# A gated long-convolution/MLP kernel on one core: sines before the filter copies, taps in one evacuation, zero matmuls on the idle TensorE, and even transforms evacuated into their own target

## Chip, cores, metric

The kernel runs on one core of a Trainium2 chip. The metric is the device time of one execution in microseconds. Each time of a kernel below is a median over several executions, slow ones included; what is said of points within a kernel comes from one profiled execution. Ratios are the mean time of one kernel's fast runs over the mean of the fast runs of the kernel before from the same rounds, with a 95% interval, so they are not quite the ratio of the medians that stand beside them. The span of a profile (first to last instruction) is about 2 us shorter than the time of the same run. A run is called slow where it is more than 1.5% above the fastest of the same kernel.

## The reference, cut to what matters

```python
x = A_q                                             # [1, 2048, 640]
g = sigmoid((x * gate_w).sum(-1, keepdims=True))
# A: 4-tap shift of k, times v, long convolution over 2048 rows with a filter per column, times q
k_shift = sum over t of k_pad[:, t:t + S] * shift_k[:, ks - 1 - t]
kv = k_shift * v
y = irfft(rfft(kv, 2S) * rfft(ssm_k, 2S))[:S] + kv * ssm_D
a = q * y
# B: MLP over the token axis
h = layernorm(x)
u = gelu(einsum("bsd,sf->bdf", h, w1) + b1)          # F = 1536
b = einsum("bdf,fs->bds", u, w2) + b2
return g * a + (1 - g) * b
```

The transform is made of matmuls with twiddle tables. The filter `ssm_k`, the product `kv` and the inverse all go through it; the MLP's first layer (512 KB loads of weights into `ring`, `X` as the other operand) and second layer (768 KB loads into `W`) fill TensorE between and behind the transforms.

## The kernel before: the parts that matter

The program is a list of operations with modelled durations. A list scheduler plays them through and fixes the order on each engine and queue; the order is then emitted, with semaphores worked out from the data dependencies. Its priorities and its `after` edges shape only the order. So a wrong duration in the model does no harm to correctness, but an engine takes its instructions in the planned order, and what the plan puts ahead goes first (in the profile after, a GELU evacuation stands behind a copy that waits 12.96 us). All matmuls are issued on one helper line (L293), all ScalarE activations on another (L667), and I tell them apart by their tiles.

The model of a DMA is short:

```python
if e in ("SP", "QA") or op.lat < 0:
    issue = 1.2 if e == "POOL" else 0.1
    s = max(t + issue, dma_free)
    dma_free = s + op.dur                      # bytes / rate, one transfer after the other
    op.end = dma_free + 2.0 + (6.0 if e == "POOL" else 0.0)
```

The front: twiddle angles (`pint`, VectorE), their sines (`FTB`, ScalarE), the filter blocks (`ssm`) transposed on TensorE and copied out (`wT`, ScalarE), the taps (`cw`), then the filter transform in 16 groups of four matmuls, each copied out by ScalarE into `C`. LayerNorm statistics of `X` follow on VectorE, and the tap matrix `KF` on GpSimd.

```python
for p in PORD:                                       # (0, 2, 1, 3)
    tt("DVE", pv, acol[p], brow, ALU.mult)           # angles as integers
    ts("DVE", pint[:, p, :, 0, :], pv, 1024.0, None, ALU.add)
    ts("DVE", pa, pa, 4095, None, ALU.bitwise_and)
    act(FTB[:, p], pa, ACT.Sin, ...)                 # cut
```

The transforms of `kv`: the even residues are evacuated into slots of another buffer (`Th`), VectorE adds them into the target, and the mixing follows.

```python
def fwd_even(src, h, dst, Th, Ts):
    for p in (0, 2): ...                             # 8 groups of two matmuls
        act(V(Th, Ts * SL + D * pos[(p, kt, c)], ...), two, ACT.Copy, vt=vt, name="Ae")
    tt_("DVE", V(dst, 0, ...), t4(0, ...), t4(2, ...), ALU.add)        # three additions
```

The middle, for the inverse transform: four DMA transposes, one for each residue `p`, read `FTB` and write `GTB`, and ScalarE gathers each back into `FTB` once the forward transforms have used that residue. `GTB` shares memory with the gate's products `gq`. The second layer's weights (`W`) are loaded on the same queue (SP).

```python
for p in range(4):
    dma(GTB[:, p], FTB[:, p], 128 * 2048, rate=200.0, transpose=True, prio=10 ** 5)
    act(V(FTB, 1024 * p, ...), V(GTB, 1024 * p, ...), ACT.Copy, prio=10 ** 5, name="gil")
for n_, hk in enumerate(HORD):
    for a in range(2):
        w2last = dma(W2h[:, 6 * a:6 * a + 6, :], dr(B_w2, ...), 128 * 6144)
```

Of the kernel before, what the change touches and what calls it, by code (L numbers as in the profile page):

```python
# [9 lines left out]
BF16 = mybir.dt.bfloat16  # L10
# [313 lines left out]
class _Sched:  # L324
# [59 lines left out]
    def run(self):  # L384
# [13 lines left out]
        free = {e: 0.0 for e in engs}  # L398
# [112 lines left out]
def _build(nc, A_q, A_k, A_v, A_shift_k, A_ssm_k, A_ssm_D, B_x, B_w1, B_b1, B_w2, B_b2, gate_w, out):  # L511
# [10 lines left out]
    with ExitStack() as es:  # L522
# [73 lines left out]
        rows = alloc("rows", [20, 4, 512], BF16, at=base_of(GT))  # L596
# [169 lines left out]
        small(rows[0:20, 0, 0:128], dr(A_shift_k, 0, [[128, 20], [1, 128]]), 5120, "QA")  # L766
        small(rows[0:4, 1, :], dr(B_b2, 0, [[512, 4], [1, 512]]), 4096, "QA")
        small(rows[0:12, 2, 0:128], dr(B_b1, 0, [[128, 12], [1, 128]]), 3072, "QA")
        for a, b in SSM0:
            ssm_load(0, a, b)  # L770
        for hk in range(4):
            x_load(hk)
        for a, b in SSM1:
            ssm_load(1, a, b)
        w1_load(0, 0)
        w1_load(0, 1)

# [9 lines left out]
        memset("POOL", cw[:, :, :], 0.0)  # L787
        ro, ri = rows[0:20, 3, :].rearrange("g (j q c) -> g j q c", j=4, q=4), V(rows, 0, [[1, 4], [0, 4], [4, 32]], pn=20)
        SC.add("DVE", 0.6, lambda s: T.op("DVE", lambda e: e.tensor_copy(ro, ri), [ri], [ro]), [ri], [ro], prio=0, name="taps")
        PORD = (0, 2, 1, 3)  # L790
        for p in PORD:
            pv = pint[:, p, :, 1, :]
            tt("DVE", pv, V(acol, p, [[4, 2], [0, 256]]), V(brow, 0, [[0, 2], [1, 256]]), ALU.mult, mode=1)
            ts("DVE", pint[:, p, :, 0, :], pv, 1024.0, None, ALU.add, mode=2)
            pa = pint[:, p, :, :, :].rearrange("q a b c -> q (a b c)")
            ts("DVE", pa, pa, 4095, None, ALU.bitwise_and, mode=2)
            act(FTB[:, p, :, :, :, :].rearrange("q a b c d -> q (a b c d)"), pa, ACT.Sin, bias=cst[:, 0:1],
                scale=-(2.0 * math.pi / 4096.0) * (1.0 - 1e-6), name="sin")
# [9 lines left out]
        for j in range(4):  # L808
            items.append(((lambda s, j=j: s[:, 512 + 20 * j:512 + 20 * j + 20]), rows[0:20, 3, 128 * j:128 * j + 128], ident[0:20, 0:20], True, True))
        mms(vt, items, prio=0, name="cst")  # L810
        for q in range(4):
            act(V(cw, q, [[7, NG], [1, 4]], p0=32 * q, pn=32), (lambda s, q=q: s[32 * q:32 * q + 32, 512:592].rearrange("p (j g) -> p g j", j=4)), ACT.Copy, vt=vt, prio=0, name="cw")
        b2f = V(cc, 0, [[1, 4], [4, 4]])
        ts("DVE", dif2[:, :], dif2[:, :], 31, None, ALU.bitwise_and, mode=2)
        ts("DVE", m32[:, :], dif2[:, :], 0.0, None, ALU.is_equal, mode=2)
# [10 lines left out]
        def transp(h, db):  # L826
            vt = _VT("cv")
            items = []
            for kt in range(2):
                for p in range(4):  # L830
                    o = (lambda s, j=4 * kt + p: s[:, 128 * j:128 * j + 128])
                    dfold = h == 0 and kt == 0 and p == 0
                    if dfold:
                        items.append((o, ident[0:1, :], Drow[0:1, 128 * db:128 * db + 128], True, False))
                    items.append((o, V(ssm, db * S + 1024 * h + 4 * kt + p, [[8, 128]]), ident[:, :], not dfold, True))
            mms(vt, items, name="wtr")
            act(V(wT, 2 * h * SL + 128 * db, [[SL, 2], [D, 4], [1, 128]]), (lambda s: s[:, :].rearrange("q (a b c) -> q a b c", a=2, b=4)), ACT.Copy, vt=vt, name="wT")

        def fwd(src, h, p, dst, slot, scale, name, neg=lambda c, k2: False):
            for k2 in range(2):  # L840
                for c in range(2):
# [5 lines left out]
                    mms(vt, items, name=name)  # L847
# [5 lines left out]
        def fwd_even(src, h, dst, Th, Ts):  # L853
            pos = {(0, 0, 0): 0, (0, 0, 1): 1, (0, 1, 0): 2, (0, 1, 1): 3, (2, 0, 1): 4, (2, 1, 0): 5, (2, 1, 1): 6, (2, 0, 0): 7}
            for p in (0, 2):
                for kt in range(2):
                    for c in range(2):
                        vt = _VT("cv")
                        items = [(chk(ci), FTB[:, p, kt, c, 0, :], src(kt, p, ci), True, True) for ci in range(2)]
                        mms(vt, items, name="A")  # L860
                        act(V(Th, Ts * SL + D * pos[(p, kt, c)], [[320, 2], [1, 320]]), two, ACT.Copy, vt=vt, name="Ae")

            def t4(o, n, dims):
                return V(Th, Ts * SL + D * o, dims + [[1, n]])
            tt_("DVE", V(dst, 0, [[2 * D, 2], [1, D]]), t4(0, 2 * D, []), t4(2, 2 * D, []), ALU.add)
            tt_("DVE", V(dst, 2 * SL + 2 * D, [[-2 * D, 2], [1, D]]), t4(4, 2 * D, []), t4(6, 2 * D, []), ALU.add)
            tt_("DVE", V(dst, D, [[2 * SL, 2], [2 * D, 2], [1, D]]), t4(0, D, [[4 * D, 2], [D, 2]]), t4(2, D, [[4 * D, 2], [D, 2]]), ALU.subtract)
# [53 lines left out]
        for h in range(2):  # L921
# [4 lines left out]
            for p in PORD:  # L926
                fwd(srcW(h), h, p, C[h], p, 1.0 / 1024.0, "W", (lambda c, k2: False) if h == 0 else (lambda c, k2: c == 1))
            if h == 0:
# [14 lines left out]
                for g0 in KFP:  # L943
                    tt("POOL", KF[:, g0:g0 + 20 // len(KFP), :, :], V(cw, 7 * g0, [[7, 20 // len(KFP)], [1, 7], [0, 32]]), V(m32, 0, [[0, 20 // len(KFP)], [0, 7], [1, 32]]), ALU.mult)
# [54 lines left out]
        fwd_even(srcA, 0, C[2], C[1], 0)  # L999
# [6 lines left out]
        fwd_even(srcB, 1, C[3], C[2], 0)  # L1006
# [252 lines left out]
```

## Time and profile before

| | |
|---|---|
| time, median | 190.22 us of the three runs that the prediction had (189.38 to 190.36); 190.00 with a fourth; 189.8 to 190.6 in the rounds of the experiments |
| span of the profile | 187.7 us |
| TensorE / VectorE / ScalarE / GpSimd busy | 93% / 90% / 64% / 20% |
| first filter matmul | 15.99 us |
| first MLP matmul | 25.54 us |
| `kv` matmuls begin | 48.41 us |
| last GELU evacuation begins | 115.28 us |

How it is read (page, chain, front, clock) stands in the prediction. This is the SP queue of the kernel before, from 70 to 110 us (start, length, line, operation and tile), and beneath it, in a second fence, how long its four transposes took to land:

```profile
79.80 13.61 SPq L260 DMA_TRANSPOSE GTB<-FTB  x4
93.45 1.20 SPq L267 DMA_DIRECT2D W<-in_B_w_dram  x2
```

```profile
DMA to landing us min/median/max: 3.0/3.2/4.7
```

### The profile page before, as it was taken

To read this page: it belongs to the slowest core of one execution; us is meant where nothing else is said; L and a number is where in the kernel's file an instruction comes from. 1 tells how busy PE (TensorE), PEld (TensorE's weight loads), DVE (VectorE), ACT (ScalarE), POOL (GpSimd) and SP (SyncE) were. 2 spreads that over 40 slices of the span, in tenths; PEclk is the share of its full clock that TensorE was granted. 3 is DMA by queue.
4 is the path that set the end of the run, shared out by engine and by line. 5 is a ranking of instruction groups with operands and counts; after the bars stand their busy time and mean duration, and the time that the engine had idled before them with its cause. 6 is when DMAs were issued, how large, how long until landed. Compare 5 with 4: busy or idle time off the path is not lost.

```text
span 187.7 us, 3316 instructions
## 1 busy us (share of the span) xinstructions
PE 173.7 (93%) x1374; PEld 129.7 (69%) x1374; DVE 168.7 (90%) x199; ACT 119.4 (64%) x180; POOL 36.9 (20%) x41
## 2 busy tenths in 40 slices
PE   3746999989999999999979999999999999999994
PEld 2523668756877786767747777888888887778673
DVE  7899795999499963999999999999999999969974
ACT  2996889599987999999798111231313224563760
POOL 2089304000000550000011530200204131252000
PEclk9999999999999999999999999999999999999999
DMA  5999999999991899990699599965967999999453
GB/s 168 400 409 370 386 218 230 365 415 193 200 338 50 196 209 231 232 201 0 132 224 271 107 191 159 341 119 170 325 124 226 303 202 248 259 211 227 138 211 138
DMA packets 38206, 42.85 MB, mean 228 GB/s; under 512 B 15787, under 2 KB 31280, under 8 KB 38192
## 3 DMA queue, kind: packets, MB, share of 16 engines
q1 hardware_dynamic: 33200, 32.15, 56.6%
q0 software_dynamic: 4928, 10.49, 31.6%
q8 instruction: 10, 0.16, 0.4%
q14 instruction: 4, 0.03, 0.0%
q10 hardware_dynamic: 64, 0.01, 0.0%
HBM read 25.87 MB, written 2.62 MB: 152 GB/s over the span
## 4 chain that ended last, share of the span: by engine, by line
PE 81%; ACT 15%; DMA 1%; issue 1%; DVE 0%
PE pp L293 81%; ACT C L667 4%; ACT wT L667 4%; ACT FTB L667 3%; ACT ksh L667 2%; DMA ssm<-in_A_ssm_k_dram 1%; ACT L667 1%; ACT GT L667 1%; ACT cw L667 0%; DVE O L679 0%; ACT gth L667 0%
## 5 line engine op out<-in xcount | busy, mean ns | idle before, releaser
L623 DVE TENSOR_TENSOR C<-C 128x2560 bf16<-128x2560 bf16 (+2 forms) x34 | 52.2, 1565 | 6.8 <-ACT C L667 6.8
L293 PE MATMUL pp<-X,ring 128*128 128x320 bf16 x384 | 55.4, 299 | 1.5 <-ACT GT L667 1.2
L293 PE MATMUL pp<-GT,W 128*128 128x320 bf16 x384 | 52.8, 299 | 0.0
L293 PEld LDWEIGHTS pp<-GT,W 128*128 128x128 bf16 x384 | 43.4, 114 | 8.8 <-ACT cgb L667 0.2
L293 PEld LDWEIGHTS pp<-X,ring 128*128 128x128 bf16 x384 | 37.2, 98 | 16.5 <-issue 1.9
L667 ACT ACTIVATE C<-pp 128x640 bf16<-128x640 f32 x64 | 40.4, 718 | 6.1 <-PE pp L293 6.0
L667 ACT ACTIVATE O<-pp,c,omg 128x640 bf16<-128x640 f32 x15 | 13.3, 884 | 34.7 <-PE pp L293 34.7
L293 PE MATMUL pp<-wT,FTB 128*128 128x320 bf16 x128 | 21.3, 323 | 2.2 <-ACT wT L667 1.4
L293 PEld LDWEIGHTS pp<-wT,FTB 128*128 128x128 bf16 x128 | 12.6, 104 | 9.7 <-ACT wT L667 1.5
L262 POOL DMA_DIRECT2D C<-C x8 | 9.9, 1359 | 47.3 <-DVE C L623 47.1
L667 ACT ACTIVATE GT<-pp,cc 128x640 bf16<-128x640 f32 x12 | 9.5, 792 | 13.0 <-PE pp L293 12.9
L262 POOL DMA_DIRECT2D C<-q_hi x6 | 5.9, 984 | 54.5 <-DVE C L623 27.6
L667 ACT ACTIVATE cgb<-pp,gg 128x640 bf16<-128x640 f32 x16 | 12.7, 794 | 5.7 <-PE pp L293 5.7
L623 DVE TENSOR_TENSOR tm<-C,C 128x2560 bf16<-128x2560 bf16 (+1 forms) x7 | 14.4, 2057 | 0.0
L899 DVE BATCH_NORM_STATS2 stats<-X 128x6 f32<-128x320 bf16 x32 | 13.4, 460 | 0.6 <-DMA X<-in_A_q_dram 0.6
L293 PE MATMUL pp<-C,FTB 128*128 128x320 bf16 x96 | 13.7, 299 | 0.0
L623 DVE TENSOR_TENSOR C<-tm 128x2560 bf16<-128x2560 bf16 (+1 forms) x10 | 12.0, 1219 | 0.0
L623 DVE TENSOR_TENSOR SS<-C 128x2560 bf16<-128x2560 bf16 x8 | 11.7, 1487 | 0.3 <-DMA C<-C 0.3
L293 PEld LDWEIGHTS pp<-C,FTB 128*128 128x128 bf16 x96 | 8.9, 98 | 4.2 <-ACT O L667 0.4
L667 ACT ACTIVATE gq<-gq 128x640 bf16<-128x640 bf16 x16 | 11.8, 748 | 0.0
L293 PE MATMUL pp<-ident,ssm 128*128 128x128 bf16 x80 | 8.4, 269 | 3.2 <-DMA ssm<-in_A_ssm_k_dram 2.2
L667 ACT ACTIVATE wT<-pp 128x1024 bf16<-128x1024 f32 x10 | 9.6, 1028 | 1.0 <-PE pp L293 1.0
(69 smaller groups left out, 183.5 us busy)
## 6 DMA issues: line engine op xcount, KB each, us to landing
ring<-in_B_w_dram SPq DMA_DIRECT2D x12, 512.0 KB, 11.1
W<-in_B_w_dram SPq DMA_DIRECT2D x8, 768.0 KB, 7.3
C<-C POOLq DMA_DIRECT2D x8, 640.0 KB, 10.3
X<-in_A_q_dram SPq DMA_DIRECT2D x4, 640.0 KB, 8.2
kn<-in_A_k_dram SPq DMA_DIRECT2D x4, 640.0 KB, 8.6
out_dram<-O SPq DMA_DIRECT2D x7, 320.0 KB, 2.8
ssm<-in_A_ssm_k_dram SPq DMA_DIRECT2D x3, 512.0 KB, 5.6
vkv<-in_A_v_dram SPq DMA_DIRECT2D x2, 640.0 KB, 5.0
```

The lines of the kernel that those rows point to most:

```text
L262: ins = engobj.dma_start(out_ap, in_ap, accum_op=ALU.add, max_dma_last_dim=2560)
L293: ins = self.nc.tensor.matmul(ps_ap, lhsT=lhsT, rhs=rhs, start=start, stop=stop, skip_group_check=True)
L623: o_ = SC.add(eng, d, lambda s: T.op(eng, lambda e: e.tensor_tensor(o, a, b, op), [a, b], [o]), [a, b], [o], prio=prio, name="tt")
L667: return T.op("ACT", lambda e: e.activation(o, src, func, **kw), rr + [src], ww)
L899: ops.append(SC.add("DVE", 0.38, (lambda o, i: lambda s: T.op("DVE", lambda e: e.bn_stats(o, i), [i], [o]))(o, i), [i], [o]))
```

## The change

The intent: bring the start of the filter transform forward (one table load less, fewer and earlier ScalarE operations ahead of it), have TensorE past its slow start by then (in the profile before, the first four filter groups take 1.07 us each and the later ones 0.62; that zero matmuls ahead of them would end this sooner was my supposition, which that profile does not show), and take from VectorE a wait in the transforms of `kv`. The core of the diff, with cuts:

```diff
-        free = {e: 0.0 for e in engs}
+        free = {e: 2.0 if e == "ACT" else 0.0 for e in engs}          # planner only
-        small(rows[0:20, 0, 0:128], dr(A_shift_k, ...), 5120, "QA")    # and b2, b1: ScalarE's queue
+        small(rows[0:20, 0, 0:128], dr(A_shift_k, ...), 5120, "SP", chain=True)   # after two ssm loads
+        zz = alloc("zz", [128, 512], BF16, at=base_of(GTB))
+        memset("DVE", zz[:, :], 0.0, prio=-1)
+        SPIN = (6, 1, 1, 1, 1)
+        def spin(k):
+            return [((lambda s: s[:, 0:512]), zz[:, 0:128], zz[:, :], True, True)] * k
...
-        for j in range(4):                                             # taps
+        for j in range(7):
-        for q in range(4):
-            act(V(cw, q, ...), (lambda s, q=q: s[32 * q:32 * q + 32, 512:592]...), ACT.Copy, ...)
+        act(cw[:, :, :], (lambda s: s[:, 512:652]...), ACT.Copy, ...)
...
+            m_ = mms(vt, (spin(SPIN[db]) if h == 0 else []) + items, name="wtr")
+            if h == 0:
+                o_.after.add(sins[0 if db == 0 else 2])                # wT behind the first sines
+                if h == 0 and p in (1, 3):
+                    sins[p].prio = SC.ops[-1].idx - (16.5 if p == 1 else 8.5)
+                    m_ = mms(vt, (spin(3) if lead else []) + items, name=name)
...
-        def fwd_even(src, h, dst, Th, Ts):
+        def fwd_even(src, h, dst):
-                        act(V(Th, Ts * SL + D * pos[(p, kt, c)], ...), two, ACT.Copy, vt=vt, name="Ae")
+                        act(V(dst, SL * (1 + p) + D * (pos[(p, kt, c)] % 4), ...), two, ACT.Copy, vt=vt, name="Ae")
...
-        fwd_even(srcA, 0, C[2], C[1], 0)
+        fwd_even(srcA, 0, C[2])
-        fwd_even(srcB, 1, C[3], C[2], 0)
+        fwd_even(srcB, 1, C[3])
```

I call the last two pieces "the even part" and everything else "the front".

More of the change, by code (lines that the diff above doesn't have):

```diff
@@ L595, in _build @@
         ksh = [alloc(f"ksh{i}", [128, 4, D], BF16, at=base_of(GT) + 5120 * (1 + i)) for i in range(2)]
-        rows = alloc("rows", [20, 4, 512], BF16, at=base_of(GT))
+        rows = alloc("rows", [20, 5, 512], BF16, at=base_of(GT))
         kn = [alloc(f"kn{i}", [128, 4, D], BF16, at=base_of(ring[1]) + 5120 * i) for i in range(2)]
@@ L765, in _build @@
         small(Drow[:, :], dr(A_ssm_D, 0, [[0, 1], [1, D]]), 1280, "QA")
-        small(rows[0:20, 0, 0:128], dr(A_shift_k, 0, [[128, 20], [1, 128]]), 5120, "QA")
-        small(rows[0:4, 1, :], dr(B_b2, 0, [[512, 4], [1, 512]]), 4096, "QA")
-        small(rows[0:12, 2, 0:128], dr(B_b1, 0, [[128, 12], [1, 128]]), 3072, "QA")
-        for a, b in SSM0:
+        for a, b in SSM0[:2]:
+            ssm_load(0, a, b)
+        small(rows[0:20, 0, 0:128], dr(A_shift_k, 0, [[128, 20], [1, 128]]), 5120, "SP", chain=True)
+        for a, b in SSM0[2:]:
             ssm_load(0, a, b)
@@ L772, in _build @@
             x_load(hk)
+        small(rows[0:4, 1, :], dr(B_b2, 0, [[512, 4], [1, 512]]), 4096, "SP", chain=True)
+        small(rows[0:12, 2, 0:128], dr(B_b1, 0, [[128, 12], [1, 128]]), 3072, "SP", chain=True)
         for a, b in SSM1:
@@ L786, in _build @@
         ts("DVE", ident[:, :], dif[:, :], 0.0, None, ALU.is_equal)
-        memset("POOL", cw[:, :, :], 0.0)
-        ro, ri = rows[0:20, 3, :].rearrange("g (j q c) -> g j q c", j=4, q=4), V(rows, 0, [[1, 4], [0, 4], [4, 32]], pn=20)
+        memset("POOL", rows[0:20, 3:5, :].rearrange("g a b -> g (a b)")[:, 0:896], 0.0)
+        ro, ri = V(rows, 1536, [[128, 4], [160, 4], [1, 32]], pn=20), V(rows, 0, [[1, 4], [0, 4], [4, 32]], pn=20)
         SC.add("DVE", 0.6, lambda s: T.op("DVE", lambda e: e.tensor_copy(ro, ri), [ri], [ro]), [ri], [ro], prio=0, name="taps")
         PORD = (0, 2, 1, 3)
+        sins = {}
         for p in PORD:
             pv = pint[:, p, :, 1, :]
-            tt("DVE", pv, V(acol, p, [[4, 2], [0, 256]]), V(brow, 0, [[0, 2], [1, 256]]), ALU.mult, mode=1)
+            t_ = tt("DVE", pv, V(acol, p, [[4, 2], [0, 256]]), V(brow, 0, [[0, 2], [1, 256]]), ALU.mult, mode=1)
             ts("DVE", pint[:, p, :, 0, :], pv, 1024.0, None, ALU.add, mode=2)
             pa = pint[:, p, :, :, :].rearrange("q a b c -> q (a b c)")
-            ts("DVE", pa, pa, 4095, None, ALU.bitwise_and, mode=2)
-            act(FTB[:, p, :, :, :, :].rearrange("q a b c d -> q (a b c d)"), pa, ACT.Sin, bias=cst[:, 0:1],
+            if p != 0:
+                t_.after.add(pprev)
+            pprev = ts("DVE", pa, pa, 4095, None, ALU.bitwise_and, mode=2)
+            sins[p] = act(FTB[:, p, :, :, :, :].rearrange("q a b c d -> q (a b c d)"), pa, ACT.Sin, bias=cst[:, 0:1],
                 scale=-(2.0 * math.pi / 4096.0) * (1.0 - 1e-6), name="sin")
@@ L807, in _build @@
         items = []
-        for j in range(4):
-            items.append(((lambda s, j=j: s[:, 512 + 20 * j:512 + 20 * j + 20]), rows[0:20, 3, 128 * j:128 * j + 128], ident[0:20, 0:20], True, True))
+        for j in range(7):
+            items.append(((lambda s, j=j: s[:, 512 + 20 * j:512 + 20 * j + 20]), V(rows, 1536 + 128 * j, [[1, 128]], pn=20), ident[0:20, 0:20], True, True))
         mms(vt, items, prio=0, name="cst")
-        for q in range(4):
-            act(V(cw, q, [[7, NG], [1, 4]], p0=32 * q, pn=32), (lambda s, q=q: s[32 * q:32 * q + 32, 512:592].rearrange("p (j g) -> p g j", j=4)), ACT.Copy, vt=vt, prio=0, name="cw")
+        act(cw[:, :, :], (lambda s: s[:, 512:652].rearrange("p (j g) -> p g j", j=7)), ACT.Copy, vt=vt, prio=0, name="cw")
         b2f = V(cc, 0, [[1, 4], [4, 4]])
-        ts("DVE", dif2[:, :], dif2[:, :], 31, None, ALU.bitwise_and, mode=2)
-        ts("DVE", m32[:, :], dif2[:, :], 0.0, None, ALU.is_equal, mode=2)
+        ts("DVE", dif2[:, :], dif2[:, :], 31, None, ALU.bitwise_and, mode=2, prio=0)
+        ts("DVE", m32[:, :], dif2[:, :], 0.0, None, ALU.is_equal, mode=2, prio=0)
         def consts():
@@ L835, in transp @@
                     items.append((o, V(ssm, db * S + 1024 * h + 4 * kt + p, [[8, 128]]), ident[:, :], not dfold, True))
-            mms(vt, items, name="wtr")
-            act(V(wT, 2 * h * SL + 128 * db, [[SL, 2], [D, 4], [1, 128]]), (lambda s: s[:, :].rearrange("q (a b c) -> q a b c", a=2, b=4)), ACT.Copy, vt=vt, name="wT")
+            m_ = mms(vt, (spin(SPIN[db]) if h == 0 else []) + items, name="wtr")
+            m_.dur = 0.5
+            o_ = act(V(wT, 2 * h * SL + 128 * db, [[SL, 2], [D, 4], [1, 128]]), (lambda s: s[:, :].rearrange("q (a b c) -> q a b c", a=2, b=4)), ACT.Copy, vt=vt, name="wT")
+            if h == 0:
+                o_.after.add(sins[0 if db == 0 else 2])
         def fwd(src, h, p, dst, slot, scale, name, neg=lambda c, k2: False):
@@ L846, in fwd @@
                             items.append((chk(ci), FTB[:, p, kt, c, k2, :], src(kt, p, ci), kt == 0, kt == 1))
-                    mms(vt, items, name=name)
+                    lead = name == "W" and (h, p, k2, c) == (0, 0, 0, 0)
+                    m_ = mms(vt, (spin(3) if lead else []) + items, name=name)
+                    m_.dur = 0.54
                     o = dst[:, slot, 2 * c + k2, :].rearrange("p (a b) -> p a b", a=2)
@@ L860, in fwd_even @@
                         mms(vt, items, name="A")
-                        act(V(Th, Ts * SL + D * pos[(p, kt, c)], [[320, 2], [1, 320]]), two, ACT.Copy, vt=vt, name="Ae")
-            def t4(o, n, dims):
-                return V(Th, Ts * SL + D * o, dims + [[1, n]])
-            tt_("DVE", V(dst, 0, [[2 * D, 2], [1, D]]), t4(0, 2 * D, []), t4(2, 2 * D, []), ALU.add)
-            tt_("DVE", V(dst, 2 * SL + 2 * D, [[-2 * D, 2], [1, D]]), t4(4, 2 * D, []), t4(6, 2 * D, []), ALU.add)
-            tt_("DVE", V(dst, D, [[2 * SL, 2], [2 * D, 2], [1, D]]), t4(0, D, [[4 * D, 2], [D, 2]]), t4(2, D, [[4 * D, 2], [D, 2]]), ALU.subtract)
+                        act(V(dst, SL * (1 + p) + D * (pos[(p, kt, c)] % 4), [[320, 2], [1, 320]]), two, ACT.Copy, vt=vt, name="Ae")
+            tt_("DVE", V(dst, 0, [[2 * D, 2], [1, D]]), V(dst, SL, [[D, 2], [1, D]]), V(dst, SL + 2 * D, [[D, 2], [1, D]]), ALU.add)
+            tt_("DVE", V(dst, 2 * SL + 2 * D, [[-2 * D, 2], [1, D]]), V(dst, 3 * SL, [[D, 2], [1, D]]), V(dst, 3 * SL + 2 * D, [[D, 2], [1, D]]), ALU.add)
+            tt_("DVE", V(dst, D, [[2 * SL, 2], [2 * D, 2], [1, D]]), V(dst, SL, [[2 * SL, 2], [D, 2], [1, D]]), V(dst, SL + 2 * D, [[2 * SL, 2], [D, 2], [1, D]]), ALU.subtract)
         def mixing(R, Th, Ts, fine=False, conj=False, prio=None):
@@ L943, in _build @@
                 for g0 in KFP:
-                    tt("POOL", KF[:, g0:g0 + 20 // len(KFP), :, :], V(cw, 7 * g0, [[7, 20 // len(KFP)], [1, 7], [0, 32]]), V(m32, 0, [[0, 20 // len(KFP)], [0, 7], [1, 32]]), ALU.mult)
+                    k_ = tt("POOL", KF[:, g0:g0 + 20 // len(KFP), :, :], V(cw, 7 * g0, [[7, 20 // len(KFP)], [1, 7], [0, 32]]), V(m32, 0, [[0, 20 // len(KFP)], [0, 7], [1, 32]]), ALU.mult)
+                    k_.after.add(pprev)
                 for hk in range(2):
```

## The prediction

> **What bounds the kernel now.** I read the page's first two parts first, then the chain of waits in order of time, then the timeline of ScalarE and TensorE in the first 34 us, then the windows table with the vector and scalar engines over the rest. The page:
>
> ```profile
> PE 173.7 (93%) x1374; PEld 129.7 (69%) x1374; DVE 168.7 (90%) x199; ACT 119.4 (64%) x180; POOL 36.9 (20%) x41
> PE   3746999989999999999979999999999999999994
> ACT  2996889599987999999798111231313224563760
> PEclk9999999999999999999999999999999999999999
> ```
>
> Each digit is 4.7 us. TensorE is short of full only in the first three slices and at the very end; ScalarE is full in the second and third. The chain of waits says the same with names:
>
> ```profile
> by line: PE pp L293 80.8%; ACT C L667 3.7%; ACT wT L667 3.6%; ACT FTB L667 2.9%; ACT ksh L667 1.8%; DMA ssm<-in_A_ssm_k_dram 1.5%; ACT L667 1.4%; ACT GT L667 1.2%; issue 0.9%; ACT cw L667 0.5%; DVE O L679 0.3%; ACT gth L667 0.1%
> ...
> 5.66 1.28 ACT L667
> 6.94 0.01 issue
> 6.96 2.19 ACT FTB L667 x2
> 9.15 0.13 ACT cw L667
> ...
> 10.09 1.02 ACT wT L667
> 11.12 2.08 ACT FTB L667 x2
> 13.19 2.75 ACT wT L667 x3
> 15.94 0.05 issue
> 15.99 11.36 PE pp L293 x64
> ```
>
> From 4.6 to 16 us ScalarE alone sets the pace: a table load, four sines (FTB), four tap evacuations (cw), five evacuations of transposed filter (wT). TensorE's first filter matmul starts at 15.99; from there the chain is 81% TensorE, and TensorE waits only 3.6 us in all (GT 2.0, wT 1.6). So whatever brings that start forward should bring the end forward, if what feeds TensorE later comes forward too. The timeline of ScalarE gives the durations:
>
> ```profile
> 2.31 1.28 ACT L667 ACT_TABLE_LOAD   x1 [2.31 <-issue]
> 4.62 1.02 ACT L667 ACTIVATE wT<-pp 128x1024 bf16<-128x1024 f32 x1 [1.02 <-PE pp L293]
> 9.06 1.01 ACT L667 ACTIVATE cw<-pp 32x80 bf16<-32x80 f32 x4
> 20.47 6.25 ACT L667 ACTIVATE C<-pp 128x640 bf16<-128x640 f32 x10 [0.36 <-PE pp L293]
> ```
>
> There are two table loads before the sines, because a copy (wT) runs ahead of them, and an evacuation of one filter group takes 0.625 us once TensorE keeps up (6.25 / 10). It does not keep up at first. The windows table, one row for each of the first groups of four matmuls:
>
> ```profile
> 15.99:17.06 1.07, 1.07 (x5) 0.60 (x6) 1.07 (x6) 0.03 (x1) 1.07 (x2) 1.00 1.08 353
> 19.20:20.27 1.07, 1.07 (x6) 0.59 (x5) 0.21 (x1) 0.70 (x1) 1.07 (x1) 1.00 1.01 399
> 20.90:21.52 0.62, 0.62 (x7) 0.46 (x5) 0.62 (x3) 0.55 (x2) 0.00 (x0) 1.00 0.96 388
> ```
>
> Four groups take 1.07 us each, then 0.62. The granted clock (the column 1.00) does not show it; the spacing does.
>
> [...] 4 x 1.07 = 4.3 us slow, four matmuls of 320 columns at 0.27 us each, later 0.136 (87.29 us / 640). [...] the filter copies after the sines need no third load before the GELU at 38.5. [...] ScalarE spends 0.31 + 0.66 us issuing three small loads before its first table load.
>
> **The change, part by part.**
>
> *One table load less, taps in one evacuation.* Removes 1.28 us, and replaces four cw copies (1.01 us together) by one of 128 x 140, which I put at 0.27 from the copy of 128 x 28 (0.21). That is 2.0 us off the ScalarE path. The tap transposes grow from 4 to 7, under 0.1 us.
>
> *Two sines move behind the start.* Only sines p=0 and p=2 precede the wT copies; p=1 and p=3 (2.18 us) are slotted among the evacuations. That brings the start forward by up to 2.2 us but returns as ScalarE work in the stage after it.
>
> *When the filter matmuls now start.* ScalarE's load begins after one DMA issue, about 1.25, and is over before the data. VectorE: the multiply 1.5 to 2.2, the two small mask operations now ahead (0.2 net), the add (0.41) and the mask (0.69) give the first sine at about 3.45. From there: 2 sines 2.19 + 5 wT at 0.95 (2.84 / 3) 4.7 + cw 0.27 = 7.2, so 10.7 if it never waits. It may wait: the second filter load lands at 5.87 and the third at 7.25 (1.65 + 5.6), and eight transposes take 1.07 cold or 0.53 warm (1.61 us / 24 later). Cold, with the leading zero matmuls, the last two blocks are ready at about 9 and 10. I take 11.3, 4.7 us before 15.99.
>
> *The zero matmuls.* Six of 512 columns, 0.43 us each cold (scaled from 0.27 for 320), fill about 1.1 to 3.7, while the first load is still in flight (3.46). They cost at most 0.3 us there. With one ahead of each block and three before the first group, they should leave at most one or two slow groups: up to 4 x (1.07 - 0.625) = 1.8 us saved, partly beside sine p=1, which holds ScalarE anyway. I count 1.2.
>
> *The stage that follows.* It is bound by ScalarE: 16 x 0.625 = 10.0, plus the two sines 2.2, plus 0.5 of start-up and the bias copy: 11.3 + 12.7 = 24.0, against 29.27 now. Then five wT of the second half, 4.75: about 28.8 against 33.9. TensorE's filler here is the first-layer matmuls, 32 by 34.3 now; they are 4.4 us and fit, because VectorE's first normalised tiles come at about 23. The second half of X is normalised by 33.4 now. VectorE's work before it is the same except for a 0.94 wait for POOL (KF held POOL until 18.3 and should now end near 17), so it comes at about 32.4, only 1 us earlier. Between 28.8 and that, TensorE has filter groups at 0.625 for 0.545 of work, a loss of about 0.4. Net at that point: 5.1 - 0.4 = 4.7 us ahead.
>
> *The even transforms evacuate into their own target* instead of another buffer. This takes away their wait for the previous mixing: VectorE sat idle 2.57 and 1.58 before the 128x1280 additions at 71.9 and 74.3. In return the odd transforms must wait for those additions, about 3.1 us (0.82 + 0.82 + 1.49), since they reuse the slots. I count nothing for TensorE, which has first-layer matmuls to fill with, and 3 to 6 us of progress for VectorE (with 2.62 of waiting at 46.9 that an earlier second half removes). VectorE needs this: its last inverse mix ends at 176.3 and TensorE uses it at 177.15, so only 0.9 us of slack.
>
> *Sum.* 4.7 ahead on TensorE, less 0.5 for new waits in the middle: 4.2 to 4.3 us. 190.2 - 4.3 = 185.9 us, 2.3% less.
>
> **The rivals.** (a) *The loads become the bound and swallow the front.* The DMA row is near full from 4 to 41 us (for 4 to 16: share 1.02, 394 GB/s), and none of these bytes are removed. For it: X limits VectorE, and the second X half and the k transposes (41.2 to 48.7) keep their time. Against it: second-half filter loads land by 16.3, and the next first-layer weights are issued at 48.7 and land in about 6.2, against first use at 71. TensorE has about 33 us of work for the 29 between. If it is right: 188 to 189. (b) *VectorE becomes the bound*, because the odd transforms now wait for its additions behind a mixing stage of 11 us. It is at 90%, and full from 97 to 160. Gain 1 to 3 us: 187.5 to 189. (c) *More is won:* the wait of 1.2 us at 97.7 for GT vanishes, the start is near 10.7, the clock is warm from the first group: 183 to 184. (d) *The zeros do not warm the clock*, because zero operands or gaps between blocks do not count: 1.2 less, about 187.
>
> **Range and chances.** (c) against (a) and (b) is nearly even around 185.9; the static order of instructions, which is planned with modelled durations, adds error either way. 8 in 10: 183.4 to 188.6. The 2% mark lies at 186.4, close below which my sum falls, so faster by over 2%: 0.58; within 2%: 0.38; slower: 0.04, since nothing is added to a busy engine but 0.3 us.
>
> **What the next profile would show.** Right: one table load before the GELU's, the first sine at 3 to 4, the first filter matmul at 10.5 to 12, at most two groups at 1.07, wT of the second half over by about 29, then TensorE as dense as before. Wrong: a first filter matmul after 13 (then ScalarE or the third filter load waits); slow groups again (d); TensorE gaps between 45 and 75 (a, or the odd transforms); VectorE with no idle time while TensorE waits for it near the end (b).

## More of the kernel before

TensorE's last 128 first-layer matmuls in the kernel before, for comparison:

```profile
97.69 17.55 PE L293 MATMUL pp<-X,ring 128*128 128x320 bf16 x128 [1.19 <-ACT GT L667]
```

ScalarE gathers the transposes, in the timeline of ScalarE:

```profile
88.02 1.36 ACT L667 ACTIVATE FTB<-GTB 128x1024 bf16<-128x1024 bf16 x1
...
99.18 2.60 ACT L667 ACTIVATE FTB<-GTB 128x1024 bf16<-128x1024 bf16 x2
102.23 0.79 ACT L667 ACTIVATE GT<-pp,cc 128x640 bf16<-128x640 f32 x1 [0.45 <-PE pp L293]
```

No gather has a bracket (the one left out, at 95.55, has none either): none of them waited. GELU evacuations (`GT`) stand between and behind them.

## The result, and the profile after

| | before | after |
|---|---|---|
| time, median of 4 | 190.00 | 196.34 (194.99 to 197.82) |
| ratio of fast runs | | 1.0338 [1.0238, 1.0439] |
| span of the profile | 187.7 | 195.5 |
| first filter matmul | 15.99 | 12.21 |
| first MLP matmul | 25.54 | 24.93 |
| `kv` matmuls begin | 48.41 | 45.86 |
| ninth GELU evacuation begins | 102.23 | 100.38 |
| last GELU evacuation begins | 115.28 | 125.08 |
| first second-layer matmul | 115.07 | 122.40 |

The kernel after is 3.4% slower, and it was *ahead* at every point of this table up to 100 us. So the main loss lies behind that. (The four times lie in two pairs, 195.0 and 195.2, 197.5 and 197.8; the profile is of a run of the upper pair.) The page of the kernel after shows it in two rows of the 40 slices, TensorE's busy tenths and its granted clock (4.9 us each):

```profile
PE   7698889989999999999999229999999999999994
...
PEclk9969999999999999999999957999999999999999
```

Slices 23 and 24 read 2 and 2 (in the kernel before both read 9), and the clock falls in slices 24 and 25 (5 and 7). The timeline of TensorE there, and that of ScalarE:

```profile
99.75 8.99 PE L293 MATMUL pp<-X,ring 128*128 128x320 bf16 x65
116.16 6.41 PE L293 MATMUL pp<-X,ring 128*128 128x320 bf16 x32 [7.41 <-ACT GT L667]
122.40 3.15 PE L293 MATMUL pp<-GT,W 128*128 128x320 bf16 x22
```

```profile
100.38 0.78 ACT L667 ACTIVATE GT<-pp,cc 128x640 bf16<-128x640 f32 x1
114.12 1.35 ACT L667 ACTIVATE FTB<-GTB 128x1024 bf16<-128x1024 bf16 x1 [12.96 <-DMA GTB<-FTB]
115.34 0.76 ACT L667 ACTIVATE GT<-pp,cc 128x640 bf16<-128x640 f32 x1
117.77 2.56 ACT L667 ACTIVATE FTB<-GTB 128x1024 bf16<-128x1024 bf16 x2 [1.67 <-DMA GTB<-FTB]
```

ScalarE stands 12.96 us in front of the first gather. The GELU evacuation that follows it in ScalarE's order stands behind it, and TensorE's MLP matmuls, whose results must be evacuated before they can go on, stop for 7.41 us. They then start on a slow clock (0.50 granted between 115 and 120 us): 32 matmuls take 6.41 us, where 128 of them took 17.55 in the kernel before (4.4 for 32), so 2.0 us more. TensorE's waits for `GT` add up to 9.2 us in the kernel after and to 2.0 in the one before. By my estimate from these figures the stall costs about 9.2 - 2.0 + 2.0 = 9.2 us. That agrees with the table: the ninth GELU evacuation was 1.85 us ahead, the second layer starts 7.3 behind, 9.2 us apart.

Why the gather waits is in the SP queue of the kernel after, and in the landing times of its transposes:

```profile
93.61 1.43 SPq L267 DMA_DIRECT2D W<-in_B_w_dram  x2
95.66 21.74 SPq L260 DMA_TRANSPOSE GTB<-FTB  x4
```

```profile
DMA to landing us min/median/max: 10.0/13.2/18.4
```

The order has turned round: the two 768 KB loads of `W` come first, and the transposes take 10.0 to 18.4 us to land where they took 3.0 to 4.7. The windows table of the kernel after, 5 us each (length; busy time of PE, PEld, DVE, ACT and POOL, with the number of instructions in brackets; granted clock, DMA share, GB/s):

```profile
100.00:105.00 5.00, 5.00 (x39) 3.60 (x37) 5.00 (x11) 0.90 (x2) 0.86 (x1) 1.00 1.06 281
105.00:110.00 5.00, 3.75 (x28) 2.46 (x26) 5.00 (x5) 0.00 (x0) 0.86 (x1) 1.00 1.38 102
110.00:115.00 5.00, 0.00 (x0) 0.00 (x0) 5.00 (x6) 0.88 (x1) 0.67 (x1) 0.82 1.31 107
115.00:120.00 5.00, 3.84 (x15) 2.23 (x16) 5.00 (x2) 3.33 (x4) 0.19 (x1) 0.50 1.29 162
```

From 105 to 115 us the DMA engines are fully taken (shares 1.38 and 1.31) and move only 102 to 107 GB/s. VectorE is full throughout, but TensorE's wait is put down to ScalarE's `GT`, and ScalarE's to the transposes.

What turned the order round? VectorE's longest waits between 40 and 100 us (total, times, longest), before and then after:

```profile
DVE C L623 <- ACT C L667: 6.8, 3, 2.6
```

```profile
DVE gq L623 <- ACT gq L667: 0.8, 1, 0.8
```

The 6.8 us of waiting for `C` are gone: 2.57 and 1.58 us stood before the additions of the even transforms, the other 2.62 at 46.9 us, ahead of them. But the gate's multiplies (`gq`) had been planned around these gaps. VectorE's mixing now runs through:

```profile
71.42 14.04 DVE L623 TENSOR_TENSOR C<-C 128x5120 bf16<-128x5120 bf16 x9
```

The multiplies start between 67 and 94 us, in place of 46 and 88. The gate's sums follow on ScalarE, twelve of the sixteen in one block from 88.4 us, and the last ends at 99.2 in place of 90.8. `gq` shares memory with `GTB`, so the transposes become ready later, at about the time when the loads of `W` are ready too (issued at 93.45 us before, straight behind the last transpose, and at 93.61 after). The transposes carry the lowest priority on that queue, and so they lost their place. (In `w2_behind` below, where no load stands ahead of it, the first transpose waits for a gate sum until 96.29 us.) That the gaps were what had kept the multiplies early is read from the timelines and not tested by itself. In `even_only` (below) the last multiply starts only 2.8 us later than before (90.4 us) and the last sum 8.4 us later (98.3), so the order planned on ScalarE has a part in the lateness as well.

The front, too, was not what I had summed. VectorE from 5 to 15 us, before:

```profile
7.51 0.69 DVE L637 TENSOR_SCALAR pint<-pint 128x1024 int32<-128x1024 int32 x1
...
8.87 1.28 DVE L899 BATCH_NORM_STATS2 stats<-X 128x6 f32<-128x320 bf16 x3 [0.57 <-DMA X<-in_A_q_dram]
```

and after:

```profile
7.39 0.69 DVE L623 TENSOR_TENSOR pint<-acol,brow 128x512 int32<-128x512 int32 x1
10.65 0.49 DVE L913 BATCH_NORM_STATS2 stats<-X 128x6 f32<-128x320 bf16 x1 [2.57 <-DMA X<-in_A_q_dram]
11.06 1.26 DVE L637 TENSOR_SCALAR pint<-pint 128x512 int32<-128x512 int32 x1
...
12.64 2.15 DVE L637 TENSOR_SCALAR pint<-pint 128x1024 int32<-128x1024 int32 x1
```

The first tile of `X` lands at 10.65, not 8.87. The plan expected it earlier and put the last two angle operations between the first statistics, so they stand behind the wait for `X`. They then run beside GpSimd's `KF` multiplies (7.81 to 16.7 us), and take 1.26 and 2.15 us in place of 0.41 and 0.69. The statistics chain ends at 24.5 us (19.4 before). TensorE, early with its filter groups, waits 1.26 us for the first normalised `X` at 24.93.

### The profile page after: what moved, and what is told of

Read it like the earlier page. It is cut to its first block, busy times and chain, and to the rows that moved or that the text cites.

```text
span 195.5 us, 3344 instructions
## 1 busy us (share of the span) xinstructions
PE 178.3 (91%) x1390; PEld 129.0 (66%) x1390; DVE 171.7 (88%) x200; ACT 117.7 (60%) x176; POOL 38.8 (20%) x41
## 3 DMA queue, kind: packets, MB, share of 16 engines
HBM read 25.87 MB, written 2.62 MB: 146 GB/s over the span
## 4 chain that ended last, share of the span: by engine, by line
PE 57%; ACT 16%; DMA 9%; DVE 8%; SPq 7%; issue 1%
PE pp L293 57%; ACT C L667 8%; SPq L260 6%; ACT gq L667 5%; DMA GTB<-FTB 5%; DVE stats L913 5%; DMA X<-in_A_q_dram 4%; ACT GT L667 2%; DVE pint L637 2%; SPq L267 1%; ACT FTB L667 1%; ACT L667 1%; DVE mv L915 1%; DVE q_hi L623 0%; DVE O L679 0%
## 5 line engine op out<-in xcount | busy, mean ns | idle before, releaser
L293 PE MATMUL pp<-X,ring 128*128 128x320 bf16 x384 | 57.2, 306 | 9.4 <-ACT GT L667 8.1
L293 PE MATMUL pp<-wT,FTB 128*128 128x320 bf16 x128 | 20.5, 310 | 1.9 <-ACT C L667 1.2
L293 PEld LDWEIGHTS pp<-wT,FTB 128*128 128x128 bf16 x128 | 11.8, 101 | 10.1 <-ACT C L667 4.1
L667 ACT ACTIVATE FTB<-GTB 128x1024 bf16<-128x1024 bf16 x4 | 5.3, 1356 | 17.5 <-DMA GTB<-FTB 17.5
L262 POOL DMA_DIRECT2D C<-q_hi x6 | 5.9, 977 | 32.4 <-DVE C L623 28.8
```

The costliest lines, as they stand in the source:

```text
L262: ins = engobj.dma_start(out_ap, in_ap, accum_op=ALU.add, max_dma_last_dim=2560)
L293: ins = self.nc.tensor.matmul(ps_ap, lhsT=lhsT, rhs=rhs, start=start, stop=stop, skip_group_check=True)
L667: return T.op("ACT", lambda e: e.activation(o, src, func, **kw), rr + [src], ww)
```

## The experiments

Twelve kernels ran, each beside the kernel before on the same chip. "Planned order kept" means that the order made for the kernel named was taken as it was and only the named operations were moved in it; "replanned" means that the scheduler ran on the edited list. The theories, with the letters that some of the expectations use (E and F are explained where they are used):

- A, the queue: ScalarE waits at the gathers because the transposes land late. A1: they land late because they stand behind the loads of `W` on one queue. A2: they land late because the gate's sums, whose memory they take, end late.
- B, the rival to the gathers being the place: taking them out of ScalarE's way only moves the stall.
- C: the even part is the origin. D, its rival: the earlier front is (everything is pulled together, and the loads meet).

| kernel | median us (runs) | ratio, 95% interval |
|---|---|---|
| even_only | 203.03 (4) | 1.0679 [1.0622, 1.0736] |
| even_undone | 189.82 (4) | 0.9969 [0.9921, 1.0017] |
| gil_last | 194.97 (4, one slow) | 1.0195 [1.0114, 1.0276] |
| w2_behind | 191.20 (4) | 1.0041 [1.0002, 1.0079] |
| rows_act | 188.52 (20) | 0.9941 [0.9916, 0.9967] |
| pint_first | 188.60 (15, three slow) | 0.9913 [0.9879, 0.9946] |
| both_front | 188.47 (15, one slow) | 0.9884 [0.9852, 0.9916] |
| both_no_zero | 189.77 (12) | 0.9990 [0.9962, 1.0017] |
| before_zero | 189.96 (4) | 1.0005 [0.9973, 1.0036] |
| gil_far | 192.31 (4, two of them slow) | 0.9987 [0.9940, 1.0035] |
| even_gil_far | 192.86 (4, one slow) | 1.0124 [1.0067, 1.0182] |
| best | 187.93 (4) | 0.9886 [0.9844, 0.9927] |

### even_undone and even_only: which part is it?

`even_undone` is the kernel after with the even transforms of the kernel before; `even_only` is the kernel before with nothing but the new even transforms. Both are replanned.

```diff
 # even_undone, against the kernel after (the calls likewise)
-        def fwd_even(src, h, dst):
+        def fwd_even(src, h, dst, Th, Ts):
-                        act(V(dst, SL * (1 + p) + D * (pos[(p, kt, c)] % 4), ...), two, ACT.Copy, ...)
+                        act(V(Th, Ts * SL + D * pos[(p, kt, c)], ...), two, ACT.Copy, ...)
```

> The changed kernel with only the even transforms put back as before (they evacuate into the other buffer). Theory C (these evacuations took away the waits of VectorE in which the gate's multiplies ran, so the gate sums finish late and the transposes fall behind the W loads): the transposes are issued before the W loads again, no long TensorE gap, 185 to 188 us. Rival D (the earlier front is enough to upset the order): still a gap of 4 us or more near 110, 192 to 197.

```diff
 # even_only, against the kernel before (the calls likewise)
-        def fwd_even(src, h, dst, Th, Ts):
+        def fwd_even(src, h, dst):
-                        act(V(Th, Ts * SL + D * pos[(p, kt, c)], ...), two, ACT.Copy, ...)
+                        act(V(dst, SL * (1 + p) + D * (pos[(p, kt, c)] % 4), ...), two, ACT.Copy, ...)
```

> The kernel before with only the even transforms changed, front as before. Theory C: the long gap appears without the new front, a ratio of 1.02 to 1.06 (194 to 201 us). Rival D: no gap, 188 to 191 us, ratio 0.99 to 1.005.

The even part alone makes the kernel before 6.8% slower, 203.03 us; without it the change is level with before, 0.9969. C holds and D falls, though both times miss C's ranges: the first is 2 us above its 194 to 201 us, the second 1.8 us above its 185 to 188, for the front gained nothing. The two traces have the mechanism in them. The SP queue of `even_only`, and TensorE at the same time:

```profile
99.26 1.44 SPq L267 DMA_DIRECT2D W<-in_B_w_dram  x1
100.75 20.69 SPq L260 DMA_TRANSPOSE GTB<-FTB  x3
```

```profile
125.05 3.36 PE L293 MATMUL pp<-GT,W 128*128 128x320 bf16 x12 [8.55 <-ACT GT L667]
```

One load of `W` stands ahead of all four of its transposes (95.23 us, with the first of them at 95.67) and a second ahead of three; they take up to 21.0 us to land, and TensorE stops for 8.55 us. In `even_undone` the transposes go first and land in 3.0 to 4.9 us, the loads follow:

```profile
86.61 7.10 SPq L260 DMA_TRANSPOSE GTB<-FTB  x4
93.76 35.67 SPq L267 DMA_DIRECT2D W<-in_B_w_dram  x6
```

No gather waits there, and the longest wait of TensorE for `GT` is 1.5 us.

### gil_last: the gathers out of the way

Kernel after, planned order kept; the four gathers behind the last GELU.

```diff
         SC.run()
+        behind([o for o in SC.order if o.name == "gil"], [o for o in SC.order if o.name == "gelu"][-1])
         SC.emit()
```

> The changed kernel with its instruction order kept, except that ScalarE's four gather copies (FTB<-GTB) stand behind its last GELU instead of among the GELUs. Theory A (a gather that waits for a late transpose holds up the GELUs behind it in ScalarE's fixed order, and TensorE with them): the 7.4 us TensorE gap near 108-116, the 0.35 us one and the slow clock after them (about 1.7 us) go, so about 186.5 to 188 us, ratio 0.98 to 0.99. Rival B (the transposes and loads themselves are what all later work waits for, so the wait only moves): 193 or more.

194.97 us, 1.0195; the verdict is unclear, for the interval takes in 2%: one run (the profiled one) took 192.54, the three others 194.79 to 195.44, of which the highest counts as slow. The stall at the GELUs is gone, but TensorE stops a little later, for an evacuation of the second layer that now stands behind the gathers:

```profile
122.65 5.53 PE L293 MATMUL pp<-GT,W 128*128 128x320 bf16 x27 [3.07 <-ACT O L667]
```

So B was right for this position, time (193 or more) and cause: the transposes still land 8.6 to 16.5 us after their issue, and whoever stands behind the gathers waits. The gathers are where it shows, not where it comes from.

### w2_behind: the queue order alone

Kernel after, planned order kept; only the first two loads of `W` moved behind the four transposes.

```diff
         SC.run()
+        behind(w2first, [o for o in SC.order if o in gtbs][-1])     # w2first: the first two W loads
         SC.emit()
```

> The changed kernel with its instruction order kept, except that on the load queue the first two W loads (768 KB each) are issued behind the four GTB transposes instead of ahead of them. If the transposes are late because they queue behind these loads (theory A1): first transpose lands within about 4 us of its buffer coming free (by 100 to 105 instead of 114), the gap shrinks to 0 to 3 us, about 187 to 190 us. If they are late because the gate sums free their buffer late (theory A2), or because they share the transfer engines with the accumulating transfers: landing moves by less than 4 us, and the time stays at 193 to 196.

191.20 us and hardly any spread (191.15 to 191.36), where the kernel after has 194.99 to 197.82: 5.1 us come back from exchanging six entries of one queue. The transposes start no earlier than in the kernel after (96.29 against 95.66), so A2, lateness by itself, is refuted, and A1 is shown: the first transpose lands at 100.3 us in place of 114.1. The time is still 1.2 us above A1's range. The SP queue and the landing times, in `w2_behind`:

```profile
96.29 9.78 SPq L260 DMA_TRANSPOSE GTB<-FTB  x4
106.12 22.96 SPq L267 DMA_DIRECT2D W<-in_B_w_dram  x6
```

```profile
DMA to landing us min/median/max: 4.0/5.5/7.7
```

ScalarE's only wait at a gather is 0.47 us. The loads of `W` are now a little late themselves: TensorE waits for them twice, 1.2 us together. GpSimd's accumulating DMAs run beside the transposes in this kernel as in the kernel after, issued within 1 us of the same times up to 106 us, so they are not what made the difference. What the order did to the landing: 13.2 us by the median behind the loads, 5.5 ahead of them. It does not explain all. The two loads had landed by 107.5 us in the kernel after, and a transpose issued at 113.83 still took 9.99 us. Why a backlog of transposes moves so little (about 105 GB/s between 105 and 115 us) stays open.

### rows_act, pint_first, both_front, both_no_zero: what the front is worth

These four start from `even_undone`, with its planned order kept, to look at the front without the stall. `rows_act` issues the three small row loads from ScalarE's queue at the start again:

```diff
-            dma(o, i, nbytes, stream=stream, **kw)
+            smalls.append(dma(o, i, nbytes, stream=stream, via="ACT", **kw))
...
+        place(smalls[1:], smalls[0], True)
```

> The version with the even transforms undone (189.8 us), its instruction order kept, except that the three small row loads are issued from ScalarE's queue at the start, as before the change. If they are what made X land at 10.5 instead of 8.9 (theory E): X lands by 9.2, the third filter load by 7.6 instead of 8.9, and the time falls by 1 to 2 us to 188 to 189. If the lateness has another source (the zero matmuls, an earlier table load): X still at 10.2 or later, same time.

`pint_first` puts the three angle operations of residue 3 ahead of the first statistics, so that they cannot stand behind the wait for `X`:

```diff
         SC.run()
+        place([t_, a_, pprev], first_stats, False)
```

> The version with the even transforms undone, its instruction order kept, except that VectorE does the last two angle operations (p=3) ahead of the first statistics of X instead of between them. Theory F (these two stand behind the wait for X and then run beside POOL's KF multiplies at 1.1 to 2.1 us instead of 0.4 and 0.7, pushing every later statistic): the chain of statistics ends about 3 us earlier (21 instead of 24.2), the first normalised X near 21 to 22, and 186.5 to 188 us. Rival: X's landing alone sets it; then the gain is under 0.7 us.

`both_front` does both.

> Both of these edits together. If E and F are the whole of why the front gained nothing: statistics end near 19.5, first layer matmul at or before 22, the second half of X normalised by 33, and the 4 us of the prediction come back, 185 to 187 us. If TensorE still gains nothing, something later (VectorE's or the loads' chain) is the bound: 188 to 190.

`both_no_zero` is that without zero matmuls:

```diff
         def spin(k):
-            return [((lambda s: s[:, 0:512]), zz[:, 0:128], zz[:, :], True, True)] * k
+            return []
```

> Both edits, and no zero matmuls (the planned durations do not count them, so the order of everything else is unchanged). If they keep the clock up for the first filter groups: without them the first three or four groups take 1.07 us and the time is 0.8 to 2 us longer than with them. If they do nothing for the end: within 0.5 us.

Against before: 0.9941, 0.9913, 0.9884 and 0.9990. `rows_act` came in its range of time but not by its mechanism (`X` at 10.14 us, where 9.2 was expected), `both_no_zero` came in as expected, and two missed: `pint_first` (186.5 to 188 expected) with statistics that end at 23.3 us, where 21 was expected, and `both_front` (185 to 187), whose 188.47 falls in its rival's range, that something later is the bound. Each of the two repairs shows a gain over `even_undone` (0.9969) that is smaller than the intervals are wide, and together they give about 0.9%, just outside them.

`pint_first` did not do it in the way I had meant. Its VectorE, and its GpSimd, at the place in question:

```profile
7.94 4.78 DVE L637 TENSOR_SCALAR pint<-pint 128x512 int32<-128x512 int32 x2
12.64 0.87 DVE L915 BATCH_NORM_STATS2 stats<-X 128x6 f32<-128x320 bf16 x2
```

```profile
7.90 8.76 POOL L623 TENSOR_TENSOR KF<-cw,m 128x1120 bf16<-128x1120 bf16 x4 [5.12 <-ACT cw L667]
```

Ahead of the wait, but beside `KF`, which starts 0.04 us earlier, the two operations take 4.78 us in place of 1.10. In `both_front` the taps are copied later and `KF` starts at 9.10; the same two operations take 1.16 us from 7.93, the statistics begin at 9.78 and TensorE's first MLP matmul at 23.51 (25.54 before). So the slowing goes with `KF`, 1.16 us alone against 4.78 beside it; by what the two engines hinder each other the profiles do not show.

In `both_front` TensorE is 4.2 us ahead at the `kv` matmuls (44.25 us), but only 1.5 us are left of it at the end, by the medians. In its profile TensorE waits, from 30 us on, 3.5 us for `GT` (2.0 before) and 0.9 for VectorE (0 before); the rest of the loss was not traced.

For the row loads the evidence is weaker. Where VectorE waited for `X`, it came at 10.5 to 11.5 us in five profiles with the rows on SP's queue, and at 8.9 to 10.3 in five fast ones with the rows on ScalarE's queue. Yet `even_only`, whose front is exactly that of the kernel before, has 10.34 where before has 8.87: single profiles scatter by 1.5 us. The early `X` of the profile that I predicted from was partly luck.

The zero matmuls are the clearest of the four: 0.9884 with them, 0.9990 without, which is 2.0 us by the ratios and 1.3 by the medians. Without them more filter groups run slow. TensorE in `both_no_zero`, then in `both_front`:

```profile
12.27 5.96 PE L293 MATMUL pp<-wT,FTB 128*128 128x320 bf16 x23 [0.47 <-ACT wT L667]
```

```profile
12.66 3.96 PE L293 MATMUL pp<-wT,FTB 128*128 128x320 bf16 x24
```

24 matmuls take 3.96 us in the one and 23 take 5.96 in the other, and the first MLP matmul comes at 23.51 us with the zeros and at 25.11 without. The 15 runs of `both_front` lie in two clusters (186.6 to 186.9 and 188.0 to 188.9, and one at 190.39); what sets them apart was not looked into.

### before_zero: the zeros on the old front

The kernel before with the zero tile and the same zero matmuls, nothing else; the order stays the same, as the zeros' modelled durations are taken off again.

```diff
+            zs = spin(SPIN[db]) if h == 0 else []
-            mms(vt, items, name="wtr")
+            m_ = mms(vt, zs + items, name="wtr")
+            m_.dur -= len(zs) * (512 / 2400.0 + 0.0025)
```

> The kernel before with nothing but the zero matmuls added (six, one ahead of each further block, three ahead of the first filter group), its order kept. If they keep the clock up on their own, the four groups of 1.07 us become at most two: 188 to 189.3 us, ratio 0.988 to 0.996. If TensorE's idle time between the blocks (1 to 2 us each while ScalarE works) lets the clock fall before the first group, or if the start is not what the end hangs on: 0.997 to 1.003.

189.96 us, 1.0005 [0.9973, 1.0036]: nothing. TensorE is idle for 1.66 and 1.44 us behind ScalarE's slow front, between 13.2 and 16.5 us, and the matmuls that follow are slow again. The kernel before has the first of these lines, `before_zero` the two others:

```profile
15.99 9.71 PE L293 MATMUL pp<-wT,FTB 128*128 128x320 bf16 x52 [1.44 <-ACT wT L667]
```

```profile
16.55 1.46 PE L293 MATMUL pp<-zz 128*128 128x512 bf16 x3 [1.44 <-ACT wT L667]
17.80 8.28 PE L293 MATMUL pp<-wT,FTB 128*128 128x320 bf16 x52
```

The three zeros ahead of the first group take 1.46 us, slow, and push it to 17.80. The 52 filter matmuls behind them take 8.28 us in place of 9.71, so 1.4 of the 1.8 us come back. So the zeros and the shorter front need each other: the mended front without zeros is worth 0.1%, zeros without the front nothing, both together 1.2%.

### gil_far, even_gil_far, best: a faster version

`gil_far` is the kernel after, planned order kept, with one gather behind each of the fourth to seventh evacuations of the second layer, where ScalarE has slack:

```diff
         SC.run()
+        gils, o1s = [o for o in SC.order if o.name == "gil"], [o for o in SC.order if o.name == "o1"]
+        for g_, o_ in zip(gils, o1s[3:7]):
+            place([g_], o_, True)
```

> The changed kernel with its order kept, but ScalarE's four gather copies moved behind the fourth to seventh output evacuation of the second layer, one behind each, well after the transposes have landed (114 to 124 us in the changed kernel) and before their first use near 157. Moving them only just behind the last GELU left a 3.1 us gap and 195 us, since the next evacuations waited instead. Theory A in its mended form (no in-order neighbour may wait for the transposes): no TensorE gap over 1 us from 100 to 150, full clock, 187.5 to 190 us. Rival (the late transposes hurt TensorE through the loads and accumulating transfers they hold up): gaps on W or on C, 191 or more.

The queue is as bad as before (9.2 to 15.4 us to land), but nobody waits for it: no gather waits, and the longest wait of TensorE after 30 us is 2.1. The two fast runs took 190.12 and 189.37, 0.9987. Two others took 194.50 and 196.05 and count as slow; I have no profile of such a run, and why they are slow stays open. So the ratio rests on two runs; `best`, with the same move, has four fast ones.

`even_gil_far` is `even_only` with the same move.

> The kernel before with the even transforms changed (203 us) and the gathers moved as in the first of these. Theory A: the stall of about 11 us is all of their cost, so 189 to 191.5 us. Rival: they also cost by making the odd transforms wait, 193 or more.

Its fast runs (191.31, 193.50, 192.22) are 1.2% above before, down from 6.8%: of what the even part costs by itself, about 10.5 us go with this move. The mean lies between the two ranges expected. The only profile is of its slow run, so I explain nothing from it, and what the remaining 1.2% are stays open.

`best` is `gil_far` with the two edits of `both_front`.

> The same, with both front edits (small rows from ScalarE's queue, the p=3 angles ahead of the statistics). If the losses are additive: 2 us below that one, 185.5 to 188 us, at least as fast as both edits with the even transforms undone (188.5). If the even transforms cost something besides the stall: 188.5 to 191.

187.93 us, 0.9886 [0.9844, 0.9927]: 1.1% below the kernel before, which is clear of the noise, and about 8 us below the kernel after. It is the lowest median of all, but its ratio is that of `both_front` (0.9884), which has the old even transforms. So, once its stall is gone, the even part is worth nothing that these runs can show.

In the profile of `best` TensorE is 5.3 us ahead of before at the `kv` matmuls (43.15 against 48.41) and 4.8 at the second layer (110.25 against 115.07), yet its span is only 2.7 shorter. TensorE, and VectorE just before it:

```profile
166.85 4.54 PE L293 MATMUL pp<-C,FTB 128*128 128x320 bf16 x32 [2.03 <-DVE C L623]
```

```profile
161.67 1.49 DVE L623 TENSOR_TENSOR SS<-C 128x2560 bf16<-128x2560 bf16 x1 [2.04 <-DMA C<-C]
```

2.03 us of the lead go there: VectorE waits for one of GpSimd's accumulating DMAs (0.3 us at the same place before), and TensorE for VectorE. 4.8 - 2.0 = 2.8 is the 2.7 that is left.

## Why the prediction was wrong

It said 185.9 us (183.4 to 188.6) with 4% for slower; the kernel took 196.34.

- *The table load, the sines, the taps.* Right. One load ahead of the GELU's, the first sine at 3.44 us (predicted 3.45), one tap copy of 0.29 us (0.27).
- *The start of the filter transform.* Right in kind, 0.9 us late: 12.21 against 11.3.
- *The zero matmuls.* Right. In the kernel after two filter groups were slow (12.21 to 14.29 us), as allowed: TensorE had waited 1.24 us for the third filter load just before, and the three zeros ahead of the first group ran slow themselves (1.46 us from 10.96). Their worth was predicted as 1.2 us and measured as 1.3 to 2.0 in `both_front`. Rival (d) is refuted: the first 24 filter matmuls took 3.96 us there with the zeros, and without them 23 took 5.96.
- *The stage that follows.* "VectorE's work before it is the same" failed. `X` landed 1.8 us later than in the profile before, two angle operations stood behind it, and these were stretched beside `KF`. The second half of `X` was normalised at 37.3 us; I had said 32.4, against 33.4 before. So the lead was 2.5 us at the `kv` matmuls, not 4.7. The repair in `both_front` and `best` gives the lead that was predicted (4.2 and 5.3).
- *The even transforms.* This is the step that failed: "I count nothing for TensorE, which has first-layer matmuls to fill with, and 3 to 6 us of progress for VectorE". The progress was there: the 4.2 us of waits at the even transforms are gone, and the 2.6 at 46.9 us that the front was to remove. The nothing for TensorE was wrong by about 9 us in the kernel after, and by about 13 us (0.0679 of 190) in the kernel with this part alone. The gate's multiplies and sums, planned around these waits, came later; later sums made later transposes, these lost their turn on the queue to 1.5 MB of weights, and ScalarE, in order, held the GELU evacuations behind a gather that waited 12.96 us.
- *The rivals.* (a) named loads, but those of the front, and looked for gaps in TensorE between 45 and 75 us; the gap came at 109. (b) named the even part as a danger, but at VectorE, and left a gain of 1 to 3 us. Neither held the queue order, for I had not listed the transfers whose consumers wait for nothing. In `best` TensorE does wait 2.0 us for VectorE at 166.85, but VectorE itself stands idle there for a DMA, so that is not (b) either.
- *The risk of a new plan.* I wrote that the static order "adds error either way" and gave slower 4%. A replan can change the order on every queue, and here the changed order of one cost more than the front won, so that was too little.

The sum as measured in the profiled runs: 2.5 us ahead at 46 us, 1.85 at 100 us, then 9.2 lost, so 7.3 behind where the second layer starts and 7.8 at the end of the span.

## What to carry to other kernels

Before changing what an engine waits for, list what fills the wait: filler work that moves later can make its memory's next user later, and on a shared queue being late can mean being behind a large load (here two of 768 KB). Read the groups that wait for *nothing*, too, and ask what they would wait for if their source came 10 us later. And put a copy that depends on a DMA where nothing urgent stands behind it, or at least keep small transfers that are waited for ahead of bulk loads on their queue (the transposes landed in 5.5 us by the median ahead of the loads, in 13.2 behind them): a planner that models a transpose as 1.3 us plus 2.0 to land (262,144 bytes at its rate of 200, which the 3.0 to 4.7 us of the kernel before agree with) cannot see that here they took 10 to 18 behind two 768 KB loads.

## What the runs measured of the hardware

- Transposes, from issue to landing: 3.0 to 3.2 us with no other transfer ahead and 4.7 with the end of a 512 KB load still in flight (both in the kernel before), 4.0 to 7.7 beside accumulating DMAs from GpSimd (`w2_behind`), 10.0 to 18.4 behind two 768 KB loads (kernel after), and up to 21.0 in `even_only`. With the queue backed up, from 105 to 115 us of the kernel after, all transfers together moved 102 to 107 GB/s.
- VectorE beside GpSimd: two VectorE integer operations took 1.16 us alone (`both_front`) and 4.78 us beside a GpSimd multiply (`pint_first`), which itself took 8.76 us in place of 8.14 for its four pieces.
- Matmuls of zeros ahead of the filter transform: 24 filter matmuls took 3.96 us behind zeros (`both_front`), and 23 took 5.96 without (`both_no_zero`). The granted clock in the trace does not always show a slow group: it read 1.00 over the slow first groups of the kernel before (1.07 us for four matmuls), and 0.50 over a group of the same speed in the kernel after.
- A table load with nothing seen behind it: the load of 1.28 us at 5.66 ends at 6.94, and the first sine starts at 6.96 in the kernel before.
